# A second form of the products, in four 32-column tiles, where TensorE already stands in column tiles

## The chip, the cores and the metric

The kernel runs on one core of a Trainium2 chip, in one launch. The metric is the device time in microseconds (us). Nine runs of the kernel before gave a median of 564.4 us (563.79 to 564.86).

## The reference, cut to what matters

Two blocks, A (attention with a memory) and B (a dense pair with ReLU), are applied twice to x of 2048 tokens by 640 features, each behind a layer norm and with a residual: `x = x + A(ln(x))`, `x = x + B(ln(x))`, and the same once more.

```
# A: 32 heads of 20, four segments of 512 tokens
q, k, v = x @ wq, x @ wk, x @ wv
for s in range(4):
    p = softmax(q_s @ k_s.T * scale + mask);  a_dot = p @ v_s
    a_mem = (phi(q_s) @ M) / (phi(q_s) @ z + 1e-6)
    o_s = g * a_mem + (1 - g) * a_dot
    M = M + phi(k_s).T @ v_s;  z = z + sum(phi(k_s))
out = concat(o_s) @ wo
# B
out = relu(x @ w1) @ w2          # 640 -> 1728 -> 640
```

`phi(t)` is t + 1 above zero and exp(t) else; the mask keeps a query from later keys.

## The kernel before, in words

All work is cut by the four segments of 512 tokens and the two layers. Every kind of work is a generator of its own (a stream), which yields operations: the scores (`scores`, L1071), their exponentials (`exps`, on ScalarE), the causal cut (`causal`, on GpSimd), the product of the probabilities with the values (`apply`, L1175), the projections (`proj_part`, L783, and `proj_v`, L836), the reading and writing of the memory M (`mem_read`, L971, and `mem_write`, L1022), the output projection (`out_proj`, L1327), and block B (`ffn`, L1381, and `ffn_rest`, L1357). Transposes between them go by DMA (`turn`, L643).

The order on each engine is fixed before the launch by a planner, `Sched` (L169). It holds a modelled clock for each engine. In each step it takes the head of every stream, works out when it could start (`_alts`, L228) and picks the one that can start first, then the one of the better priority (`run`, L267). A TensorE operation carries a modelled duration (`mm_ns`, L346: columns / 2.4 + 2.6 ns) and a form: `full`, `rows` or `cols`. The planner keeps the form in which TensorE stands in `self.mode` and adds `SWITCH_NS` (96 ns, L158) to an operation of another form. An operation with a `lag` (`COLS_LAG`, 1500 ns, L159) is put off in `_late` (L247) as long as the form is `full` and it has not been ready for that long.

The three forms:

- `rows`: the scores (L1093). A head has 20 features, so four heads lie at partitions 0, 32, 64 and 96, and their matmuls use four row groups of the array. 160 such operations, two for each pair of PSUM slots, until all 64 groups of heads are through.
- `cols`: the product with the values (L1187) of four heads and the last 64 columns of w1 (L1367). Each matmul has at most 32 weight columns and writes PSUM partitions 0, 32, 64 or 96 and up; four of them lie side by side in the array. A round is four matmuls, one in each column tile.
- `full`: all the rest, with 128 weight columns. The products go through the helper `group` (L606): k = 0 is L613, the other k are L616, and one operation of the planner is one matmul, so that scores can come between two k. `mem_read` (L984) and `mem_write` (L1036) issue two or three matmuls as one operation. `apply_by_token` (L1226) is the product with the values in the first eight groups, with 21 moving columns.

A matmul in the source is two instructions on TensorE, a weight load (the profile's engine PEld) and the matmul (PE). Only the last matmul of an operation tells a semaphore.

Of the kernel before, what the change touches and what calls it, by code (L numbers as in the profile page):

```python
# [109 lines left out]
class Op:  # L110
# [4 lines left out]
    def __init__(self, alts, waits, dma=None, acq=None, urgent=False, take=(), mode="full", lag=0.0, port=False):  # L115
        self.lag = lag
        self.port = port
        self.alts = alts
        self.mode = mode
        self.acq = acq  # L120
        self.waits = [t for t in waits if t is not None]
        self.dma = dma
        self.urgent = urgent
        self.take = take
# [44 lines left out]
class Sched:  # L169
# [54 lines left out]
    def _pick(self, slots):  # L224
        return min((s for s in slots if s.free), default=None,
                   key=lambda s: max([self.at(t) for t in s.tks], default=0.0))

    def _alts(self, op):  # L228
        res = []
        waits = op.waits  # L230
        if op.acq is not None:
            s = self._pick(op.acq)
            if s is None:
                return res
            waits = waits + s.tks
        for k, (e, hold, fns, tail) in enumerate(op.alts):
            m = PE_MARGIN if e == "pe" else 0.0
            if e == "pe" and op.mode != self.mode:
                hold = hold + SWITCH_NS
            start = max([self.at(t) + SEM_NS + m for t in waits], default=0.0)  # L240
            start = max(self.free[e], start)
            if e == "dve" and op.port and self.free["pool"] > start:
                hold = max(hold, self.free["pool"] - start + PORT_NS)
            res.append((start + hold, start, k, e))
        return res
# [21 lines left out]
    def run(self):  # L267
        while True:
# [40 lines left out]
            _, st, end, start, k, op = best  # L309
            e, hold, fns, tail = op.alts[k]  # L310
            if e == "pe":
                self.mode = op.mode
            waits, slot = op.waits, None
            for s in op.take:
                s.free = False
# [25 lines left out]

def pe(ns, fns, waits=(), acq=None, take=(), mode="full", lag=0.0):
    return Op([("pe", ns, fns, 190.0)], waits, acq=acq, take=take, mode=mode, lag=lag)


def mm_ns(n):  # L346
    return max(26.0, n / 2.4 + 2.6)
# [29 lines left out]
def bass_interleave_layers__memory_aug_infini_attn__dense_activation_relu__prompt_kernel(  # L377
    nc, A_x, A_wq, A_wk, A_wv, A_wo, A_beta, B_x, B_w1, B_w2, out,
):
    with contextlib.ExitStack() as es:  # L380
# [225 lines left out]
        def group(slots, n, mms, waits):  # L606

            bk = tk = None
            last = len(mms) - 1
            for k, (a, b, *w) in enumerate(mms):  # L610
                w = list(w[0]) if w else []
                if k == 0:
                    bk, tk = yield pe(mm_ns(n), [(lambda e, bk, a=a, b=b: e.matmul(  # L613
                        bk.ap[:, 0:n] if len(b.shape) == 2 else bk.ap[:, 0:n].rearrange("p (i n) -> p i n", n=128), a, b, start=True, stop=(last == 0)), last == 0)], list(waits) + w, acq=slots)
                else:
                    tk = yield pe(mm_ns(n), [(lambda e, k=k, a=a, b=b, bk=bk: e.matmul(  # L616
                        bk.ap[:, 0:n] if len(b.shape) == 2 else bk.ap[:, 0:n].rearrange("p (i n) -> p i n", n=128), a, b, start=False, stop=(k == last)), k == last)], w)
            return bk, tk


# [208 lines left out]
        def vx(a, s):  # L829

            return 2 if (a, s) == (0, 0) else s % 2
# [139 lines left out]
        def mem_read(hb):  # L971
            def f(a, s):
# [6 lines left out]
                lst = [(c, max(CH_H0[c], 16 * hb), min(CH_H1[c], 16 * hb + 16)) for c in range(FC)]  # L979
                lst = [x for x in lst if x[1] < x[2]]  # L980
                for i in range(NJ):
                    fns = []
                    for z, (c, h0, h1) in enumerate(lst):
                        fns.append((lambda e, bk, c=c, h0=h0, h1=h1, z=z, i=i: e.matmul(  # L984
                            bk.ap[:, (h0 - 16 * hb) * 21:(h1 - 16 * hb) * 21],
                            phs[:, c * L + i * 128:c * L + (i + 1) * 128],
                            BD[:, CH_OFF[c] + (h0 - CH_H0[c]) * 21:CH_OFF[c] + (h1 - CH_H0[c]) * 21],
                            start=(z == 0), stop=True, skip_group_check=True), z == len(lst) - 1))
                    bk, tk = yield pe(60.0 * len(lst), fns, phi + bdt, acq=MISC if (a, s) == (0, 1) else MISC[:1])
                    rm = yield Acq(RMEM[hb])  # L990
                    om = bk.ap[:, 0:336].rearrange("p (h e) -> p h e", e=21)
                    ta = yield dve(16, 1, lambda e, rm=rm, om=om: e.tensor_scalar(
# [29 lines left out]
        def mem_write(a, s):  # L1022
            mg = yield Need("maskg")
            if s < NSEG - 1:
# [3 lines left out]
                for p, cs in enumerate(PARTS):  # L1028
# [2 lines left out]
                    w = CH_OFF[cs[-1] + 1] - o0  # L1031
                    bk = None
                    for i in range(NJ):
                        fns = []
                        for c in cs:
                            fns.append((lambda e, b=None, c=c, i=i, o0=o0, st=(i == 0 and c == cs[0]), bk=bk: e.matmul(  # L1036
                                (b or bk).ap[:, CH_OFF[c] - o0:CH_OFF[c + 1] - o0], phk[:, c, i, :],
                                VAUG[vx(a, s)][:, i, CH_H0[c]:CH_H1[c], :].rearrange("p h e -> p (h e)"),
                                start=st, stop=True, skip_group_check=True), i == NJ - 1 and c == cs[-1]))
                        if i == 0:  # L1040
                            bk, lastd = yield pe(66.0 * len(cs), fns, pht + vt, acq=MISC)
                        else:
                            lastd = yield pe(66.0 * len(cs), fns)
                    if s == 0:
                        tu = yield dve(w, 1, lambda e, bk=bk, o0=o0, w=w: e.tensor_copy(
                            M_sb[:, o0:o0 + w], bk.ap[:, 0:w]), [lastd] + S.events.get(("BD", a - 1, NSEG - 2), []))
# [468 lines left out]
```

## Time and profile before

| | us |
|---|---|
| median of nine runs | 564.4 |
| the profiled execution | 565.46 |
| its span, first to last instruction | 563.7 |
| TensorE matmuls busy, 5212 of them | 554.3 |
| weight loads busy, 5212 | 298.2 |
| VectorE busy | 410.1 |
| ScalarE busy | 410.9 |
| GpSimd busy | 193.2 |
| products of `group` with w2, 320 columns (L616, x768), busy | 124.3 |
| products of `group` with w1, 512 columns (L616, x416), busy | 113.6 |

Times in the profile are those of one execution. PE is TensorE's matmuls, PEld its weight loads, DVE is VectorE, ACT is ScalarE, POOL is GpSimd, SP issues most DMAs. A row of a group names line, engine, operation, what is written and read, and the shape of one; 128\*32 means 128 rows and 32 weight columns, 128x512 means 128 partitions by 512 columns that stream through. Matmuls are pipelined: a duration holds the way through the array and several matmuls are under way at once. How dense they lie is read from the starts of one and the next in the timeline. In the section on DMA queues a row has packets, MB and share. The chain that ended last is followed back from the last instruction, at each step to what released it.

### The profile page before, as it was taken

Reading aid. Unit: us, or ns where it says so; the run is one execution under the profiler, and the core shown is the slowest. Engines: PE = TensorE matmul, PEld = TensorE weight load, DVE = VectorE, ACT = ScalarE, POOL = GpSimd, SP = SyncE. Lnnn points to the kernel's source line nnn. Section 1 sums busy time; section 2 is a strip of 40 time slices with the busy share of each in tenths; the row PEclk is TensorE's granted clock in tenths of the full one; section 3 lists DMA queues with packets and bytes.
Section 4 is the critical chain, followed back from the end, with each engine's and each line's share of the span. In section 5 each row is a group of like instructions: output and inputs, shape, how many; then the busy total and the mean of one; then the engine's idle time right before and its main releaser. Section 6 shows DMA issues by size and latency. Waiting matters only on the chain.

```text
span 563.7 us, 12825 instructions
## 1 busy us (share of the span) xinstructions
PE 554.3 (98%) x5212; PEld 298.2 (53%) x5212; DVE 410.1 (73%) x1054; ACT 410.9 (73%) x522; POOL 193.2 (34%) x302
## 2 busy tenths in 40 slices
PE   8998999999999999999999999999999999999998
PEld 7554554455554445645445544465445654655655
DVE  4967988998998788899588985588867876452202
ACT  5699889889779878797799787678877678323140
POOL 5345334333444344344333442044421433101000
PEclk9999999999999999999999999999999999999999
DMA  8596998845374417363277141871329311532101
GB/s 267 129 229 162 220 192 190 227 87 89 74 173 90 85 51 162 60 127 53 75 171 139 20 68 37 200 131 28 56 67 215 80 44 20 93 67 59 37 0 48
DMA packets 129980, 60.92 MB, mean 108 GB/s; under 512 B 108802, under 2 KB 119810, under 8 KB 129922
## 3 DMA queue, kind: packets, MB, share of 16 engines
q1 hardware_dynamic: 129504, 59.62, 47.3%
q8 instruction: 41, 0.67, 0.5%
q10 hardware_dynamic: 418, 0.49, 0.3%
q14 instruction: 17, 0.14, 0.1%
HBM read 20.57 MB, written 12.85 MB: 59 GB/s over the span
## 4 chain that ended last, share of the span: by engine, by line
PE 84%; DVE 6%; DMA 5%; ACT 2%; SPq 1%; issue 1%; POOL 0%
PE ps L616 55%; PE ps L613 11%; PE ps L1093 8%; PE ps L1187 6%; DMA otk<-otu 2%; PE ps L984 1%; PE ps L1036 1%; DMA pad<-scr 1%; PE ps L1226 1%; ACT PT L1155 1%; DVE o_sb L1281 1%; PE ps L1367 1%; DMA x_sb<-in_A_x_dram 1%; DVE stats L624 1%; DMA beta_bc<-in_A_beta_dram 1%
## 5 line engine op out<-in xcount | busy, mean ns | idle before, releaser
L1155 ACT ACTIVATE PT<-ps 128x1024 bf16<-128x1024 f32 x320 | 309.0, 1026 | 59.7 <-PE ps L1093 53.7
L1167 POOL TENSOR_SCALAR_AFFINE_SELECT PT<-PT 128x512 bf16<-128x512 bf16 x256 | 167.7, 673 | 265.5 <-ACT PT L1155 265.5
L616 PE MATMUL ps<-w_r,hT 128*128 128x320 bf16 x768 | 124.3, 299 | 0.0
L616 PE MATMUL ps<-xnT,w_r 128*128 128x512 bf16 x416 | 113.6, 379 | 0.0
L1309 DVE TENSOR_TENSOR x_sb<-x_sb,ps 128x320 bf16<-128x320 bf16 x128 | 60.7, 480 | 71.2 <-PE ps L616 70.1
L616 PEld LDWEIGHTS ps<-w_r,hT 128*128 128x128 bf16 x768 | 72.5, 98 | 33.1 <-issue 5.8
L1093 PE MATMUL ps<-pad 20*128 20x512 bf16 (+3 forms) x1024 | 63.4, 301 | 1.9 <-DMA pad<-scr 0.9
L616 PEld LDWEIGHTS ps<-xnT,w_r 128*128 128x128 bf16 x416 | 39.3, 98 | 43.0 <-issue 3.9
L624 DVE BATCH_NORM_STATS2 stats<-x_sb 128x6 f32<-128x320 bf16 x124 | 55.5, 473 | 3.5 <-DMA x_sb<-in_A_x_dram 3.0
L1396 ACT ACTIVATE hT<-ps 128x512 bf16<-128x512 f32 x56 | 33.5, 599 | 22.7 <-PE ps L616 22.1
L616 PE MATMUL ps<-wo_r,oT 128*128 128x320 bf16 x256 | 46.2, 300 | 0.0
L1093 PEld LDWEIGHTS ps<-pad 20*128 20x128 bf16 x1024 | 17.9, 92 | 52.5 <-ACT PT L1155 26.2
L1394 DVE TENSOR_SCALAR hT<-ps 128x512 bf16<-128x512 f32 x48 | 32.7, 683 | 11.7 <-PE ps L616 11.5
L1187 PE MATMUL ps<-PT,v_aug 128*21 128x128 bf16 (+3 forms) x896 | 40.5, 301 | 0.0
L613 PE MATMUL ps<-xnT,w_r 128*128 128x512 bf16 x104 | 39.6, 381 | 0.3 <-DVE om_sb L995 0.3
L1197 DVE CAST otu<-ps 128x512 bf16<-128x512 f32 x46 | 31.4, 682 | 9.0 <-PE ps L1187 8.7
L640 POOL TENSOR_TENSOR rstd<-lnU,mhalf 128x2 f32<-128x2 f32 (+2 forms) x26 | 20.6, 791 | 46.1 <-DVE lnU L636 35.9
L616 PE MATMUL ps<-wv_r,xnT 128*128 128x320 bf16 x192 | 36.2, 300 | 0.0
L616 PE MATMUL ps<-xnT,wk_r 128*128 128x512 bf16 (+1 forms) x128 | 34.9, 366 | 0.0
L616 PE MATMUL ps<-xnT,wq_r 128*128 128x512 bf16 (+1 forms) x128 | 34.0, 366 | 0.0
L950 ACT ACTIVATE stg<-stg 128x512 bf16<-128x512 bf16 x50 | 31.4, 634 | 3.4 <-DVE rtmp L948 3.4
L951 DVE TENSOR_TENSOR phs<-stg,rtmp 128x512 bf16<-128x512 bf16 x50 | 23.7, 474 | 10.3 <-ACT stg L950 9.6
(108 smaller groups left out, 683.1 us busy)
## 6 DMA issues: line engine op xcount, KB each, us to landing
pad<-scr SPq DMA_DIRECT2D x124, 80.0 KB
scr<-stg SPq DMA_DIRECT2D x34, 256.0 KB, 3.0
out_dram<-x_sb SPq DMA_DIRECT2D x16, 160.0 KB, 1.8
w_r<-in_B_w_dram SPq DMA_DIRECT2D x10, 216.0 KB, 2.7
w_r<-in_B_w_dram SPq DMA_DIRECT2D x13, 160.0 KB, 3.0
x_sb<-in_A_x_dram SPq DMA_DIRECT2D x10, 160.0 KB, 3.6
scr<-w_r SPq DMA_DIRECT2D x5, 256.0 KB, 3.0
wv_r<-in_A_wv_dram SPq DMA_DIRECT2D x1, 800.0 KB, 8.4
```

Of the source, the lines that this page charges most:

```text
L613: bk, tk = yield pe(mm_ns(n), [(lambda e, bk, a=a, b=b: e.matmul(bk.ap[:, 0:n] if len(b.shape) == 2 else bk.ap[:, 0:n].rearrange("p (i n) ...
L616: tk = yield pe(mm_ns(n), [(lambda e, k=k, a=a, b=b, bk=bk: e.matmul(bk.ap[:, 0:n] if len(b.shape) == 2 else bk.ap[:, 0:n].rearrange("p (i ...
L624: tk = yield dve(320, 1, lambda e, c2=c2: e.bn_stats(stats6[:, t % 12, c2, :], x_sb[:, t, c2 * 320:(c2 + 1) * 320]), xt)
L950: te = yield act(512, lambda e, q=q: e.activation(q, q, ACT.Exp), [tr] + p, psum=False)
L1093: fns.append([(lambda e, z=z, j=j, hh=hh, N=N, o=o, sl=sl, q=hh % 2: e.matmul(slot.ap[:, q, o:o + N], sl.ap[32 * hh:32 * hh + DH, z, 0, 12 ...
L1155: tx = yield act(1024, lambda e, dst=dst, src=src: e.activation(dst, src, ACT.Exp, scale=SCALE), sc + pw)
L1167: tm = yield pool(600.0, lambda e, reg=reg: e.affine_select(out=reg, in_=reg, pattern=[[0, 4], [1, 128]], compare_op=ALU.is_ge, fill=0.0, ...
L1187: fns.append((lambda e, OD, j=j, hh=hh: e.matmul(OD.ap[32 * hh:32 * hh + DH + 1, 128 * j:L], VAUG[vx(a, s)][:, j, 4 * g + hh, :], pt.ap[:, ...
L1197: te = yield evac(L, 1, lambda e: e.tensor_copy(dst, OD.ap), lambda e: e.activation(dst, OD.ap, ACT.Copy), [tk] + OTU[0].tks)
L1309: ta = yield dve(320, 1, lambda e: e.tensor_tensor(x_sb[:, t, 320 * hf:320 * hf + 320], x_sb[:, t, 320 * hf:320 * hf + 320], bk.ap[:, 0:32 ...
L1394: th = yield evac(512, 1, lambda e, dc=dc, bk=bk: e.tensor_scalar(hT[:, dc, :], bk.ap[:, :], 0.0, None, ALU.max), lambda e, dc=dc, bk=bk: ...
L1396: lambda e, dc=dc, bk=bk: e.activation(hT[:, dc, :], bk.ap[:, :], ACT.Relu), [tk] + HT.tks)
```

## The change

The planner's operation gets a second list of instructions, `cols`. An operation that has one has no form of its own: `_mode` gives it the form in which TensorE stands, unless that is `rows`, where it is `full`. So it never counts as a change of form behind a full or a column operation. When the planner takes it while TensorE stands in columns, `op.cols` is issued instead of the full list. `quarters` cuts the 128 weight columns into four of 32 with their 32 PSUM partitions; each quarter is a matmul with all 128 rows and the same moving columns. The products of `group`, `mem_read` and `mem_write` get this second form. `apply_by_token`, the transposes and the scores keep theirs. The planner's duration is the same for both forms, and the semaphore is told by the last quarter.

```diff
--- before.py
+++ after.py
@@ -117,6 +117,7 @@
         self.port = port
         self.alts = alts
         self.mode = mode
+        self.cols = None
         self.acq = acq
         self.waits = [t for t in waits if t is not None]
         self.dma = dma
@@ -225,6 +226,11 @@
         return min((s for s in slots if s.free), default=None,
                    key=lambda s: max([self.at(t) for t in s.tks], default=0.0))
 
+    def _mode(self, op):
+        if op.cols is None:
+            return op.mode
+        return self.mode if self.mode != "rows" else "full"
+
     def _alts(self, op):
         res = []
         waits = op.waits
@@ -235,7 +241,7 @@
             waits = waits + s.tks
         for k, (e, hold, fns, tail) in enumerate(op.alts):
             m = PE_MARGIN if e == "pe" else 0.0
-            if e == "pe" and op.mode != self.mode:
+            if e == "pe" and self._mode(op) != self.mode:
                 hold = hold + SWITCH_NS
             start = max([self.at(t) + SEM_NS + m for t in waits], default=0.0)
             start = max(self.free[e], start)
@@ -309,7 +315,10 @@
             _, st, end, start, k, op = best
             e, hold, fns, tail = op.alts[k]
             if e == "pe":
+                op.mode = self._mode(op)
                 self.mode = op.mode
+                if op.mode == "cols" and op.cols is not None:
+                    fns = op.cols
             waits, slot = op.waits, None
             for s in op.take:
                 s.free = False
@@ -341,6 +350,15 @@
 
 def pe(ns, fns, waits=(), acq=None, take=(), mode="full", lag=0.0):
     return Op([("pe", ns, fns, 190.0)], waits, acq=acq, take=take, mode=mode, lag=lag)
+
+
+def either(op, cols):
+    op.cols = cols
+    return op
+
+
+def quarters(a):
+    return [(slice(32 * c, 32 * c + 32), a[:, 32 * c:32 * c + 32]) for c in range(4)]
 
 
 def mm_ns(n):
@@ -607,14 +625,29 @@
 
             bk = tk = None
             last = len(mms) - 1
+
+            def view(ap, b):
+                return ap[:, 0:n] if len(b.shape) == 2 else ap[:, 0:n].rearrange("p (i n) -> p i n", n=128)
+
             for k, (a, b, *w) in enumerate(mms):
                 w = list(w[0]) if w else []
+
+                def mm(e, dst, k=k, a=a, b=b):
+                    return e.matmul(view(dst.ap, b), a, b, start=(k == 0), stop=(k == last))
+
+                def quarter(e, dst, rows, part, k=k, b=b):
+                    return e.matmul(view(dst.ap[rows], b), part, b, start=(k == 0), stop=(k == last))
+
                 if k == 0:
-                    bk, tk = yield pe(mm_ns(n), [(lambda e, bk, a=a, b=b: e.matmul(
-                        bk.ap[:, 0:n] if len(b.shape) == 2 else bk.ap[:, 0:n].rearrange("p (i n) -> p i n", n=128), a, b, start=True, stop=(last == 0)), last == 0)], list(waits) + w, acq=slots)
+                    fns = [(mm, last == 0)]
+                    cols = [(lambda e, dst, rows=rows, part=part, q=quarter: q(e, dst, rows, part), last == 0 and c == 3)
+                            for c, (rows, part) in enumerate(quarters(a))]
+                    bk, tk = yield either(pe(mm_ns(n), fns, list(waits) + w, acq=slots), cols)
                 else:
-                    tk = yield pe(mm_ns(n), [(lambda e, k=k, a=a, b=b, bk=bk: e.matmul(
-                        bk.ap[:, 0:n] if len(b.shape) == 2 else bk.ap[:, 0:n].rearrange("p (i n) -> p i n", n=128), a, b, start=False, stop=(k == last)), k == last)], w)
+                    fns = [(lambda e, bk=bk, mm=mm: mm(e, bk), k == last)]
+                    cols = [(lambda e, bk=bk, rows=rows, part=part, q=quarter: q(e, bk, rows, part), k == last and c == 3)
+                            for c, (rows, part) in enumerate(quarters(a))]
+                    tk = yield either(pe(mm_ns(n), fns, w), cols)
             return bk, tk
 
 
@@ -979,14 +1012,19 @@
                 lst = [(c, max(CH_H0[c], 16 * hb), min(CH_H1[c], 16 * hb + 16)) for c in range(FC)]
                 lst = [x for x in lst if x[1] < x[2]]
                 for i in range(NJ):
-                    fns = []
+                    fns, cols = [], []
                     for z, (c, h0, h1) in enumerate(lst):
-                        fns.append((lambda e, bk, c=c, h0=h0, h1=h1, z=z, i=i: e.matmul(
-                            bk.ap[:, (h0 - 16 * hb) * 21:(h1 - 16 * hb) * 21],
-                            phs[:, c * L + i * 128:c * L + (i + 1) * 128],
-                            BD[:, CH_OFF[c] + (h0 - CH_H0[c]) * 21:CH_OFF[c] + (h1 - CH_H0[c]) * 21],
-                            start=(z == 0), stop=True, skip_group_check=True), z == len(lst) - 1))
-                    bk, tk = yield pe(60.0 * len(lst), fns, phi + bdt, acq=MISC if (a, s) == (0, 1) else MISC[:1])
+                        def mm(e, bk, rows, part, c=c, h0=h0, h1=h1, z=z):
+                            return e.matmul(
+                                bk.ap[rows, (h0 - 16 * hb) * 21:(h1 - 16 * hb) * 21], part,
+                                BD[:, CH_OFF[c] + (h0 - CH_H0[c]) * 21:CH_OFF[c] + (h1 - CH_H0[c]) * 21],
+                                start=(z == 0), stop=True, skip_group_check=True)
+                        qt = phs[:, c * L + i * 128:c * L + (i + 1) * 128]
+                        fns.append((lambda e, bk, mm=mm, qt=qt: mm(e, bk, slice(0, 128), qt), z == len(lst) - 1))
+                        for y, (rows, part) in enumerate(quarters(qt)):
+                            cols.append((lambda e, bk, mm=mm, rows=rows, part=part: mm(e, bk, rows, part),
+                                         z == len(lst) - 1 and y == 3))
+                    bk, tk = yield either(pe(60.0 * len(lst), fns, phi + bdt, acq=MISC if (a, s) == (0, 1) else MISC[:1]), cols)
                     rm = yield Acq(RMEM[hb])
                     om = bk.ap[:, 0:336].rearrange("p (h e) -> p h e", e=21)
                     ta = yield dve(16, 1, lambda e, rm=rm, om=om: e.tensor_scalar(
@@ -1031,16 +1069,22 @@
                     w = CH_OFF[cs[-1] + 1] - o0
                     bk = None
                     for i in range(NJ):
-                        fns = []
+                        fns, cols = [], []
                         for c in cs:
-                            fns.append((lambda e, b=None, c=c, i=i, o0=o0, st=(i == 0 and c == cs[0]), bk=bk: e.matmul(
-                                (b or bk).ap[:, CH_OFF[c] - o0:CH_OFF[c + 1] - o0], phk[:, c, i, :],
-                                VAUG[vx(a, s)][:, i, CH_H0[c]:CH_H1[c], :].rearrange("p h e -> p (h e)"),
-                                start=st, stop=True, skip_group_check=True), i == NJ - 1 and c == cs[-1]))
+                            def mm(e, b, rows, part, c=c, i=i, o0=o0, st=(i == 0 and c == cs[0])):
+                                return e.matmul(
+                                    b.ap[rows, CH_OFF[c] - o0:CH_OFF[c + 1] - o0], part,
+                                    VAUG[vx(a, s)][:, i, CH_H0[c]:CH_H1[c], :].rearrange("p h e -> p (h e)"),
+                                    start=st, stop=True, skip_group_check=True)
+                            end = i == NJ - 1 and c == cs[-1]
+                            fns.append((lambda e, b=None, bk=bk, mm=mm, kt=phk[:, c, i, :]: mm(e, b or bk, slice(0, 128), kt), end))
+                            for y, (rows, part) in enumerate(quarters(phk[:, c, i, :])):
+                                cols.append((lambda e, b=None, bk=bk, mm=mm, rows=rows, part=part: mm(e, b or bk, rows, part),
+                                             end and y == 3))
                         if i == 0:
-                            bk, lastd = yield pe(66.0 * len(cs), fns, pht + vt, acq=MISC)
+                            bk, lastd = yield either(pe(66.0 * len(cs), fns, pht + vt, acq=MISC), cols)
                         else:
-                            lastd = yield pe(66.0 * len(cs), fns)
+                            lastd = yield either(pe(66.0 * len(cs), fns), cols)
                     if s == 0:
                         tu = yield dve(w, 1, lambda e, bk=bk, o0=o0, w=w: e.tensor_copy(
                             M_sb[:, o0:o0 + w], bk.ap[:, 0:w]), [lastd] + S.events.get(("BD", a - 1, NSEG - 2), []))
```

## The prediction

> **What bounds the kernel now.** I read the page first: the shares of the engines, then the chain that ended last.
>
> ```profile
> PE 554.3 (98%) x5212; PEld 298.2 (53%) x5212; DVE 410.1 (73%) x1054; ACT 410.9 (73%) x522; POOL 193.2 (34%) x302
> PE 84%; DVE 6%; DMA 5%; ACT 2%; SPq 1%; issue 1%; POOL 0%
> q8 instruction: 41, 0.67, 0.5%
> ```
>
> TensorE is busy 98% of the span, and 84% of the chain runs through it. Its idle time is 563.7 - 554.3 = 9.4 us, and the waits of TensorE (another view) show no place over 1.6 us. The granted clock is 9 or more in every slice. So what counts is how tightly matmuls follow each other, and that is in the starts, since matmuls overlap and their durations say little. The timeline of TensorE (start us, us, line, what) has all three forms side by side:
>
> ```profile
> 371.77 0.40 PE L1093 MATMUL ps<-pad 20*128 20x384 bf16 x8
> 372.10 0.72 PE L1187 MATMUL ps<-PT,v_aug 128*21 128x512 bf16 x16
> 372.75 0.31 PE L613 MATMUL ps<-wo_r,oT 128*128 128x320 bf16 x1
> 372.90 0.71 PE L616 MATMUL ps<-wo_r,oT 128*128 128x320 bf16 x4
> 373.44 0.30 PE L613 MATMUL ps<-wo_r,oT 128*128 128x320 bf16 x1
> 373.58 0.71 PE L616 MATMUL ps<-wo_r,oT 128*128 128x320 bf16 x4
> 374.12 0.30 PE L616 MATMUL ps<-w_r,hT 128*128 128x320 bf16 x1
> 374.26 0.30 PE L613 MATMUL ps<-wo_r,oT 128*128 128x320 bf16 x1
> 374.49 0.40 PE L1093 MATMUL ps<-pad 20*128 20x512 bf16 x4
> 374.82 0.72 PE L616 MATMUL ps<-wo_r,oT 128*128 128x320 bf16 x4
> ```
>
> Full products of 320 columns follow at 0.54 us for four, 136 ns each (single starts: 135 to 136; of 512 columns 215 to 216, of 147 columns 63 to 69). Where the form changes, time is lost: from the last product at 374.26 to the scores at 374.49 are 0.23 us, 96 ns more than the 136. The trace has 394 changes of form: 152 full to rows, 118 rows to full, 54 columns to full, 42 rows to columns, 20 full to columns, 8 columns to rows. Wherever no semaphore is in between, the start comes 95 to 96 ns later than the last matmul's own width would give (231 against 136, 311 against 216; 151 against 56 after the 128-column matmul that ends L1187). That is a tenth of a microsecond each, some 38 us in all.
>
> The column form stands in the trace too:
>
> ```profile
> 457.54 0.30 PE L616 MATMUL ps<-w_r,hR 128*128 128x320 bf16 x1
> 457.77 0.73 PE L1367 MATMUL ps<-xnT,w_r 128*32 128x256 bf16 x20
> 458.32 0.72 PE L1187 MATMUL ps<-PT,v_aug 128*21 128x512 bf16 x16
> 458.97 0.40 PE L1093 MATMUL ps<-pad 20*128 20x384 bf16 x8
> ```
>
> L1367 is just what the change makes of a product: 128 rows, 32 weight columns, four tiles, new weights for each. Its 20 matmuls are five rounds of four and take 0.55 us to the next column operation. The single starts say how: four within 10 ns, the next four 108 to 109 ns after the first four. The full form at 256 columns has 109 (L616, 23 times). In L1187 a round of 384 columns takes 162 to 163 ns, which is 384 / 2.4 + 2.5. Between L1367 and L1187 nothing is lost, since the form stays.
>
> **The change part by part.**
>
> *Changes of form removed.* After a column operation the products now stay in columns until the next scores. Each of the 54 changes columns to full goes: "columns, full, rows" becomes "columns, rows", one stall of 96 ns instead of two. In the tail (the last scores are at 481.4, the last L1187 at 486.8) no scores come any more, so TensorE stays in columns to the end, and the two L1367 there (495.5, 530.9) lose their change into columns as well. 56 x 96 ns = 5.4 us. The skew of 10 ns at the end of a column run is paid once, as before.
>
> *The products' own pace.* From column operations to the next scores the trace has 597 matmuls of the kinds touched (265 of 512, 252 of 320, 80 of the memory, L984 and L1036), in runs of mostly 8 to 15, and 452 in the tail (322 of 320, 130 of 512): 1049 of 2740 take the new form if the order stays. By the rows of L1367 and L1187 a round costs what the full matmul costs, so I take nothing for them. What the trace doesn't show is this form kept up for long. A 320 product becomes 4 weight loads and 4 matmuls in 136 ns, 34 ns a pair. The nearest row is L1226: 40 pairs at 25 ns each (53.48 to 54.50 in the timeline) right behind a wait that had ended 0.2 us before. From below: nothing is gained, since width / 2.4 is the same. From above: the densest stretch of 100 pairs is 41.04 to 45.27, 4.23 us, 42 ns a pair. Were that the limit, a 320 product would take 169 ns, 33 more: 322 x 33 = 10.6 us in the tail, 252 x 33 = 8.3 us before it; 512 products (216) would not feel it. I take 0, by L1226, and keep the upper end as a rival.
>
> [...]
>
> *Memory products.* 58 of 147 columns, 10 of 168 and 12 of 84 follow a column operation. Their full pace is 64, 72 and 37 ns, so 8 instructions would have to pass in that time. Below: 0, as the last round of L1187 (four of 128 columns) is followed 151 ns later, no more than width and switch. Above: four times L1226's 25 ns, 100 ns a round: 58 x 36 + 10 x 28 + 12 x 63 = 3.1 us. I take 0, the row nearest in shape, and keep 3.1 us in the range.
>
> [...]
>
> *Instruction fetch.* 1049 x 6 = 6300 more instructions for TensorE. 41 fetches of 16 KB carry the 10424 weight loads and matmuls and their waits now, some 256 each; each took 0.9 to 1.5 us. At 17 ns an instruction 256 last 4.4 us, so a fetch still fits. Cover gone, each would cost up to 1 us, 14 of them in the tail. At 374.83 a fetch starts and the matmuls after it keep their 136 ns: it is ahead of need. I take 0.
>
> *The order.* The planner sees no switch cost in columns, and its lag of 1500 ns for column operations holds only in full form; a second column operation in a run may come earlier. A few changes of form more or less: 5 x 96 = 0.5 us either way. ScalarE (104 of 137 us busy in 350 to 487) and VectorE (232 of 270 us in 80 to 350) have room for 1% more pace.
>
> *What comes back as waits.* Between the layers (336 to 361) TensorE waits 1.25 us in four places for DVE and a DMA (0.20, 0.17, 0.33, 0.55). Those chains don't get shorter, and some of what was saved before ends in them. I take 0.5 us.
>
> Sum: -5.4 + 0.5 = **-4.9 us**. The profiled execution took 565.46 us around its span of 563.7; it would be 560.6, span 558.8. The median of the nine runs is 564.4, so the forecast is **559.5**.
>
> **Rivals.**
>
> *A. The gain is swallowed.* Some 40 of the 58 column runs lie before 348, 3.8 us. If the latency between the layers takes all of it, 1.6 us are left: 562.8. For it: the chain runs through DMA otk<-otu at 336.9 (4.8 us) and o_sb after it. Against: TensorE is fed with other work there and shows 1.25 us of idle. With the memory rounds at 100 ns (+3.1) it would be no change, 564 to 565.
>
> *B. Issue becomes the bound, slower.* In columns four times the instructions pass per product; place: the 72 us tail without a break, then each run. It decides from 34 ns a pair on. If 42 ns a pair is all that lasts, the tail alone costs 10.6 us: 564.4 + 10.6 - 4.9 = 570; with the runs before (8.3) and the memory rounds at 169 ns (80 x 104 = 8.3) 587. For it: no stretch of the trace beyond 40 pairs is as dense. Against: L1226, and the four starts within 10 ns.
>
> *C. It does not happen.* If the planner puts a product first after scores, TensorE is in full form and nothing changes: 564.4. Against: 42 of 62 entries into columns come straight from scores.
>
> **How the numbers follow.** Forecast 0.64, its own range 557.5 to 562.6 (a few switches more saved; the memory rounds at 3.1). A 0.13, C 0.03, B 0.20. About 0.2% (1.1 us) is what a measurement can tell from no change: faster, below 563.3, is the forecast and a third of A, 0.68; same 0.12; slower 0.20. The range 557.3 to 566.5 holds the forecast, A, C and the mildest of B, and leaves out most of B: some 8 in 10.
>
> **What would show it.** Right: changes columns to full near 0, columns to rows near 60; in the tail products of 320 columns at 136 ns a round, in fours within 10 ns; TensorE's pairs at about 8400; changes of form some 56 fewer. Wrong: rounds of 320 over 140 ns in the tail (B), gaps of about 1 us every 256 instructions (fetch), memory rounds at 100 ns, or the same starts before 336 to 361 and longer waits in it (A).

## The result and the profile after

The changed kernel takes **559.33 us** (median of 10 runs, 558.27 to 560.05), beside 564.50 us for the kernel before (31 runs, 563.72 to 567.04): the ratio is 0.9901, with a 95% interval of 0.9892 to 0.9910. The profiled execution took 559.42 us around a span of 557.7; before it was 565.46 around 563.7. So 5.2 us went by the medians and 6.0 by the spans of the two profiled executions; 4.9 had been forecast. (One execution on record, the profiled one of e1_order_only, stood at a granted clock of 0.64 and took 803.86 us; without it that kernel's median would be 564.2 instead of 564.35.)

The same three lines of the page as before: TensorE's busy time and instructions, the chain of waits by engine, the queue of the instruction fetches (packets of 16 KB, MB, share).

```profile
PE 547.5 (98%) x8257; PEld 308.4 (55%) x8257; DVE 422.5 (76%) x1077; ACT 400.0 (72%) x499; POOL 194.1 (35%) x302
...
q8 instruction: 65, 1.06, 0.8%
...
PE 90%; DVE 4%; DMA 3%; ACT 1%; SPq 1%; POOL 1%; issue 0%; ACTq 0%
```

TensorE passes 8257 pairs of weight load and matmul instead of 5212, its instructions come in 65 fetches instead of 41, and its share of the chain grew. Busy 98% hides the gain: idle was 9.4 us and is 10.2. What went is time *between* the starts, which the busy time counts as busy. It shows in the timeline of TensorE (start us, us, line, what), behind column operations:

```profile
453.03 0.40 PE L1137 MATMUL ps<-pad 20*128 20x384 bf16 x8
453.36 0.72 PE L1231 MATMUL ps<-PT,v_aug 128*21 128x512 bf16 x16
453.91 1.03 PE L639 MATMUL ps<-xnT,w_r 128*32 128x512 bf16 x16
454.77 0.34 PE L1018 MATMUL ps<-BD,phs 128*32 128x84 bf16 x12
454.95 0.39 PE L639 MATMUL ps<-xnT,w_r 128*32 128x512 bf16 x4
```

L1231 is the apply, L1187 of the kernel before. There the product began 0.65 us after it (372.10 to 372.75); here it begins 0.55 us after it (453.36 to 453.91). It is now L639, four matmuls of 32 columns for one of 128. Sixteen of them, four rounds of 512, take 0.86 us to the next operation, 215 to 216 ns each as in the full form. L1018, a memory read of three chunks, issues 12 matmuls in the 0.18 us that its chunks need anyway.

In the tail no scores come any more, and the columns stay to the end:

```profile
482.00 1.94 PE L639 MATMUL ps<-w_r,hT 128*32 128x320 bf16 x52
483.76 0.31 PE L639 MATMUL ps<-w_r,hR 128*32 128x320 bf16 x4
483.90 1.94 PE L639 MATMUL ps<-w_r,hT 128*32 128x320 bf16 x52
...
489.47 0.31 PE L639 MATMUL ps<-w_r,hR 128*32 128x320 bf16 x4
489.60 0.72 PE L1411 MATMUL ps<-xnT,w_r 128*32 128x256 bf16 x20
...
552.85 1.94 PE L639 MATMUL ps<-w_r,hT 128*32 128x320 bf16 x52
554.62 0.31 PE L639 MATMUL ps<-w_r,hR 128*32 128x320 bf16 x4
```

From 482.00 to 483.90 are 14 rounds of 320 columns (52 + 4 matmuls): 1.90 us, 136 ns a round, the full form's pace. It is the same 70 us later, and L1411 starts without a change of form.

Counted in the trace, the changes of form are 339 instead of 394: none from columns to full (54 before), 55 from columns to rows (8), 105 from full to rows (152), 123 from rows to full (118), 37 from rows to columns (42), 19 from full to columns (20). Where a full or a column run ends, the start still comes 93 to 96 ns later than the last matmul's own width would give; behind scores it is 88 to 101 ns. 55 x 96 ns = 5.3 us. (What a change costs in all is more, 111 ns; see e5_alternate.) The waits of TensorE (what waited for what: us in all, times, longest) moved, and did not grow in sum. Two rows of the kernel before, then five of the changed one, the last from its timeline:

```profile
PE ps L1093 <- DMA pad<-scr: 0.9, 2, 0.5
PE ps L1093 <- ACT PT L1155: 0.8, 2, 0.6
...
PE ps L616 <- POOL mhalf L566: 1.6, 1, 1.6
PE ps L1137 <- DMA pad<-scr: 1.1, 1, 1.1
PE ps L1137 <- ACT PT L1199: 0.9, 2, 0.6
PE ps L636 <- DVE w_r L834: 0.9, 1, 0.9
...
365.93 0.39 PE L1137 MATMUL ps<-pad 20*128 20x512 bf16 x4 [1.13 <-DMA pad<-scr]
```

Added up over the trace (whatever a start is late beyond the width of the matmul before it and the 96 ns of a change), the waits are 10.9 us, against 11.1 before. Of the four waits between the layers (336 to 361) three are gone. The fourth, scores behind pad's DMA, has moved and grown: the same scores waited 0.55 us at 360.80 before and wait 1.20 us at 365.93 now, counted alike (the row shows 1.13, without the part under the matmul before). In sum that is 1.25 us before and 1.20 now.

### The profile page after: what moved, and what is told of

Read it like the earlier page. It is cut to its first block, busy times and chain, and to the rows that moved or that the text cites. A ratio compares the mean times of both kernels' runs of the same rounds, so it can differ in the third digit from the quotient of the medians.

```text
span 557.7 us, 18924 instructions
## 1 busy us (share of the span) xinstructions
PE 547.5 (98%) x8257; PEld 308.4 (55%) x8257; DVE 422.5 (76%) x1077; ACT 400.0 (72%) x499; POOL 194.1 (35%) x302
## 3 DMA queue, kind: packets, MB, share of 16 engines
q8 instruction: 65, 1.06, 0.8%
## 4 chain that ended last, share of the span: by engine, by line
PE 90%; DVE 4%; DMA 3%; ACT 1%; SPq 1%; POOL 1%; issue 0%; ACTq 0%
PE ps L636 44%; PE ps L639 26%; PE ps L1137 9%; PE ps L1231 6%; PE ps L1075 1%; PE ps L1270 1%; PE ps L1018 1%; ACT PT L1199 1%; DMA otk<-otu 1%; DMA pad<-scr 1%; PE ps L1411 1%; DVE stats L657 1%; DVE hT L1438 1%; DVE xn_tok L703 1%; DMA beta_bc<-in_A_beta_dram 1%; POOL rstd L673 0%
## 5 line engine op out<-in xcount | busy, mean ns | idle before, releaser
L636 PE MATMUL ps<-w_r,hT 128*128 128x320 bf16 x470 | 75.1, 300 | 0.0
L636 PE MATMUL ps<-xnT,w_r 128*128 128x512 bf16 x276 | 68.6, 380 | 0.0
L639 PE MATMUL ps<-xnT,w_r 128*32 128x512 bf16 x976 | 59.4, 379 | 0.3 <-DVE hT L1438 0.3
L636 PEld LDWEIGHTS ps<-w_r,hT 128*128 128x128 bf16 x470 | 43.6, 98 | 22.4 <-issue 5.7
L639 PE MATMUL ps<-w_r,hT 128*32 128x320 bf16 x1448 | 55.3, 299 | 0.0
L639 PEld LDWEIGHTS ps<-w_r,hT 128*32 128x32 bf16 x1448 | 38.1, 97 | 10.8 <-DVE x_sb L1353 0.3
L1438 DVE TENSOR_SCALAR hT<-ps 128x512 bf16<-128x512 f32 x57 | 38.9, 684 | 6.3 <-PE ps L636 5.7
L1231 PE MATMUL ps<-PT,v_aug 128*21 128x128 bf16 (+3 forms) x896 | 40.4, 301 | 0.4 <-DVE hT L1438 0.4
L636 PEld LDWEIGHTS ps<-xnT,w_r 128*128 128x128 bf16 x276 | 24.6, 97 | 28.2 <-issue 4.8
L639 PEld LDWEIGHTS ps<-xnT,w_r 128*32 128x32 bf16 x976 | 25.3, 97 | 21.3 <-DVE hT L1438 0.5
L636 PE MATMUL ps<-wv_r,xnT 128*128 128x320 bf16 x180 | 33.9, 300 | 0.0
L834 DVE CAST stg<-ps 128x512 bf16<-128x512 f32 x42 | 28.5, 683 | 6.2 <-PE ps L636 5.6
```

Of the source, the lines that this page charges most:

```text
L636: return e.matmul(view(dst.ap, b), a, b, start=(k == 0), stop=(k == last))
L639: return e.matmul(view(dst.ap[rows], b), part, b, start=(k == 0), stop=(k == last))
L834: te = yield evac(N, 1, lambda e, sg=sg, bk=bk: e.tensor_copy(sg.ap[:, t0:t0 + N], bk.ap[:, 0:N]), lambda e, sg=sg, bk=bk: e.activation(sg ...
L1231: fns.append((lambda e, OD, j=j, hh=hh: e.matmul(OD.ap[32 * hh:32 * hh + DH + 1, 128 * j:L], VAUG[vx(a, s)][:, j, 4 * g + hh, :], pt.ap[:, ...
L1438: th = yield evac(512, 1, lambda e, dc=dc, bk=bk: e.tensor_scalar(hT[:, dc, :], bk.ap[:, :], 0.0, None, ALU.max), lambda e, dc=dc, bk=bk: ...
```

## The experiments

Theory S: what pays is the 55 stalls; the column form itself runs at the full form's pace. Rival O: the planner now believes that TensorE stands in columns, so it puts operations in another order, and the order brings the gain. L636 is the full form of a product, L639 the column form; both plan and form are set at one place in the planner's commit (the two lines at "fns = op.cols").

**The new order alone (e1_order_only).** The plan of the changed kernel, the full form always. By the order of the changed kernel that makes 398 changes of form.

```diff
-                if op.mode == "cols" and op.cols is not None:
-                    fns = op.cols
```

> The changed kernel's plan and order on every engine, but every product is issued in full form, so TensorE changes form 398 times instead of 339. Theory (the gain is the stalls of 96 ns at changes of form): 559.3 + 59 x 0.096 = 565.0 us, within 0.5. Rival (the gain comes from the new order, the planner seeing fewer switches): 559.3, as the changed kernel. Rival (the column form itself is quicker per product): between the two, by less than 96 ns a change.

Measured: 564.35 us, ratio 0.9998 (0.9986 to 1.0009), 0.65 below S's number and just outside its 0.5. The order alone gives nothing: O falls.

**The forms alone (e2_forms_only).** The plan of the kernel before; a product is issued in columns where the engine, as tracked beside the plan, stands in columns. 336 changes.

```diff
-        return self.mode if self.mode != "rows" else "full"
+        return op.mode
...
-                op.mode = self._mode(op)
                 self.mode = op.mode
-                if op.mode == "cols" and op.cols is not None:
+                stands = getattr(self, "stands", "full")
+                if op.cols is None:
+                    self.stands = op.mode
+                elif stands == "cols":
                     fns = op.cols
+                else:
+                    self.stands = "full"
```

> The plan and the order of the kernel before on every engine, but a product is issued in columns when TensorE already stands in columns: 336 changes of form instead of 394. Theory (stalls): 564.5 - 58 x 0.096 = 558.9 us, within 0.7. Rival (order): 564.5, no change from before.

Measured: 561.63 us, ratio 0.9953 (0.9936 to 0.9970): 2.8 us gained where 5.6 were expected. Both were too simple. The 58 stalls went, but half of what they were worth came back. Two places in its profile say where: counted as the 10.9 and 11.1 us above, TensorE waits 7.6 us for VectorE, against 5.4 in the kernel before and 5.6 in the changed one, and the clock falls once. The windows view (window, its length, busy us and instructions of PE, PEld, DVE, ACT, POOL, then granted clock, DMA share, GB/s):

```profile
52.40:56.00 3.60, 3.02 (x61) 1.57 (x61) 2.44 (x8) 3.60 (x5) 2.66 (x5) 1.00 0.62 183
56.00:59.50 3.50, 3.10 (x10) 0.81 (x11) 2.65 (x7) 2.82 (x4) 2.57 (x4) 0.57 0.93 230
59.50:63.00 3.50, 3.50 (x60) 2.14 (x59) 3.15 (x11) 2.70 (x4) 0.64 (x1) 0.94 1.05 275
```

0.57 in the window after a wait of 0.88 us for VectorE: half speed for 3.4 us, some 1.7 us lost. Two of its six runs show this; without them the median is 561.3. So of the 5.2 us some 2 come only with the forms *and* the plan made for them together.

**Another tile shape (e4_two_64_tiles).** Two tiles of 64 columns in place of four of 32. Entered from four tiles of 32, that is a change of shape, though both are column tiles. (In three more places, not shown, the last tile that tells the semaphore is c == 1 instead of c == 3.)

```diff
-    return [(slice(32 * c, 32 * c + 32), a[:, 32 * c:32 * c + 32]) for c in range(4)]
+    return [(slice(64 * c, 64 * c + 64), a[:, 64 * c:64 * c + 64]) for c in range(2)]
```

> The changed kernel's plan and order, but the second form has two tiles of 64 weight columns instead of four of 32. Where the stall belongs to a change of the tile's shape, 32 to 64 columns is a change too, 398 in all: 559.3 + 59 x 0.096 = 565.0. Where it belongs only to going between full and column tiles, 559.3.

Measured: 565.0 us, ratio 1.0011 (1.0002 to 1.0021), S's number: all of the gain is gone. Its timeline:

```profile
455.75 0.73 PE L1411 MATMUL ps<-xnT,w_r 128*32 128x256 bf16 x20
456.41 0.41 PE L639 MATMUL ps<-xnT,w_r 128*64 128x512 bf16 x2
...
457.25 0.72 PE L1231 MATMUL ps<-PT,v_aug 128*21 128x512 bf16 x16
457.90 1.05 PE L639 MATMUL ps<-xnT,w_r 128*64 128x512 bf16 x8
```

0.65 us from the apply to the product (457.25 to 457.90), as in the kernel before, not the 0.55 of the changed kernel. What costs the stall is a change of the tiles' shape; every pair of shapes that follow each other in these kernels shows it (93 to 96 ns, behind scores 88 to 101). This is the sharpest test of S: plan, order and columns are those of the changed kernel, and only the shape differs.

**More changes (e5_alternate).** Every second product that would be in columns is issued full: 1288 changes, 949 more than in the changed kernel.

```diff
                 if op.mode == "cols" and op.cols is not None:
-                    fns = op.cols
+                    self.turn = not getattr(self, "turn", False)
+                    if self.turn:
+                        fns = op.cols
```

> The changed kernel's plan and order, but of the product operations that it issues in columns every second one is issued in full form: 1288 changes of form instead of 339, with the same work. Theory (each change costs a stall of 96 ns on the path): 559.3 + 949 x 0.096 = 650.4 us, within 5. Rival (a change costs only where it meets the scores, the rest is hidden by weight loads): under 600.

Measured: 661.29 us, ratio 1.1718 (1.1703 to 1.1733): 10.9 above S's 650.4 and outside its 5, far from the rival's 600. (661.3 - 559.3) / 949 = 107 ns a change, 11 more than S's 96. The timeline has them singly:

```profile
600.15 0.31 PE L638 MATMUL ps<-w_r,hT 128*128 128x320 bf16 x1
600.39 0.32 PE L641 MATMUL ps<-w_r,hT 128*32 128x320 bf16 x4
600.64 0.31 PE L638 MATMUL ps<-w_r,hT 128*128 128x320 bf16 x1
600.88 0.32 PE L641 MATMUL ps<-w_r,hT 128*32 128x320 bf16 x4
```

0.49 us for a pair of products that take 0.27 in one form: 0.22 for two changes, 110 ns each. The 11 ns are no cost of lone rounds, they stand at every change of the kernel before too, outside the 96. There the first full product behind a change is followed after 146 ns (372.75 to 372.90) and the later ones after 136; in the median of 170 such runs it is 10 ns more. And the four matmuls of a round start over 9 to 10 ns: in a run of rounds the next four start 125 to 126 ns after the last of the four before, so this skew is paid once, at the run's end. Counted from the first start of a run to the first start of the next, less what its matmuls need (columns / 2.4 + 2.5 ns, four side by side counted once), a change takes 111 ns in the median, in the kernel before, in the changed kernel and here. By that 949 changes are 105 us; the waits are 2.9 us shorter (8.0 against 10.9).

**Products only (e7_helper_only).** The memory operations keep the full form only; 350 changes.

```diff
-                    bk, tk = yield either(pe(60.0 * len(lst), fns, phi + bdt, acq=MISC if (a, s) == (0, 1) else MISC[:1]), cols)
+                    bk, tk = yield pe(60.0 * len(lst), fns, phi + bdt, acq=MISC if (a, s) == (0, 1) else MISC[:1])
...
-                            bk, lastd = yield either(pe(66.0 * len(cs), fns, pht + vt, acq=MISC), cols)
+                            bk, lastd = yield pe(66.0 * len(cs), fns, pht + vt, acq=MISC)
...
-                            lastd = yield either(pe(66.0 * len(cs), fns), cols)
+                            lastd = yield pe(66.0 * len(cs), fns)
```

> Only the products of the helper have the second form; the memory products (reading and writing) stay full. 350 changes of form instead of 339. Theory (stalls): 559.3 + 11 x 0.096 = 560.4. Rival (memory rounds in columns are slower than full ones, up to 36 ns each at about 80 rounds): 557 to 559, quicker than the changed kernel.

Measured: 563.42 us, ratio 0.9978 (0.9964 to 0.9992), 4.1 us above the changed kernel; neither number. 11 more changes are 1.06 us, and the waits in its profiled execution (562.09 us) are 1.1 us longer (12.0 against 10.9): together 2.2 of the 2.3 us by which its span is longer. Its median is another 1.3 above that execution, which is not settled. Without memory rounds in columns the kernel is slower, not faster; as the plan differs as well, that alone would not exclude a small cost of them. Their starts in the changed kernel do: 63 to 69 ns apart for 147 columns, as in the full form.

**Columns always (e3_all_columns).** The planner and the issue both take columns for every product, so that full form is left only to what has no other: 12016 column matmuls, 335 changes.

```diff
-        return self.mode if self.mode != "rows" else "full"
+        return "cols"
```

> Every product of the helper and of the memory in columns, behind scores too: 12016 column matmuls instead of 5116, 335 changes of form against 339. Theory (stalls, the form itself is free however long it lasts): 559.3 - 4 x 0.096 = 558.9, and up to 1 us either way for the other order. Rival (issue or instruction fetch becomes the bound when columns are kept up, above all in the first 80 us, where the DMA queues are 0.8 busy): over 563.

Measured: 573.13 us, ratio 1.0162 (1.0137 to 1.0187): the theory's 558.9 missed by 14 us, on the rival's side of 563, although within a run no round is slower (320 columns: 135 to 136 ns). The waits:

```profile
PE ps L1137 <- ACT PT L1199: 5.7, 8, 1.7
...
PE ps L639 <- issue: 1.4, 2, 0.8
```

Scores wait eight times for ScalarE's exponential (0.9 us in the changed kernel). "Columns" in the plan also switches off the lag of 1500 ns that holds a column operation back while TensorE is in full form. Two changes had been mixed; the next two kernels part them.

**Columns always, on the changed kernel's plan (e8_all_columns_same_order).** 334 changes.

```diff
-                if op.mode == "cols" and op.cols is not None:
+                if op.cols is not None:
                     fns = op.cols
```

> The changed kernel's plan and order on every engine, but every product in columns, behind scores too: 12016 column matmuls, 334 changes of form instead of 339. Theory (the form costs nothing, e3_all_columns lost its time through its other plan): 559.3 - 5 x 0.096 = 558.8, within 1. Rival (columns kept up cost time by issue or fetch): over 565, near the 573.1 of e3_all_columns.

**The plan of "columns always", form by where the engine stands (e9_plan_of_all_columns).** 375 changes, 4624 column matmuls; in effect the edits of e2_forms_only and e3_all_columns together.

> The plan and order of e3_all_columns, in which the lag of the column operations never holds, but products behind scores are issued full: 375 changes of form, 4624 column matmuls. Theory (the plan of e3_all_columns is what cost there): 573.1 + 40 x 0.096 = 577 us, within 2. Rival (the columns kept up were the cost): 559.3 + 36 x 0.096 = 562.8.

Measured: 567.21 us for the first, ratio 1.0047 (1.0032 to 1.0062), 7.9 above the changed kernel; 570.02 for the second, ratio 1.0101 (1.0088 to 1.0114), 10.7 above it, between its theory's 577 and its rival's 562.8. The second's 36 more changes are 3.5 us (4.0 at 111 ns), so its plan costs some 7, with the same waits for ScalarE:

```profile
PE ps L1141 <- ACT PT L1203: 5.5, 8, 1.8
```

Four of these eight waits (3.6 us) lie between 114 and 122, and behind them the clock is halved from 120.4 to 127.3; all four executions show a mean granted clock of 0.993 or 0.994. TensorE works 5.6 us of that time, so some 2.8 of the 7 us are the clock's. 7.9 + 7 above 559.3 is 574, beside 573.1 measured for both at once. So a plan that never holds column operations back costs 7 us here; no run parts the lag from the change of form that this plan no longer counts. The other 7.9 us, with the plan held fixed, are the rival's "columns kept up": waits of TensorE in e8_all_columns_same_order, two places of its timeline, and the last row of its windows:

```profile
PE ps L1137 <- DMA pad<-scr: 3.5, 2, 2.0
PE ps L639 <- issue: 2.9, 4, 1.2
```
```profile
15.25 0.50 PE L639 MATMUL ps<-xnT,wq_r 128*32 128x256 bf16 x10 [1.22 <-issue]
...
382.83 0.72 PE L639 MATMUL ps<-w_r,hT 128*32 128x320 bf16 x13
384.40 0.59 PE L639 MATMUL ps<-w_r,hT 128*32 128x320 bf16 x11 [0.85 <-issue]
...
59.50:63.00 3.50, 3.50 (x40) 1.01 (x32) 2.51 (x6) 2.57 (x3) 1.71 (x4) 0.58 1.09 242
```

"issue" is a stall for which no semaphore accounts. At 384.40 it falls *inside* a round: 13 matmuls, a stall, 11 matmuls. There are five of one kind (15.25, 43.06, 314.11, 379.24, 384.40), 3.7 us in all by the starts, and counted in TensorE's stream of instructions they stand at 449, 1729, 14785, 17858 and 18113: apart by multiples of 256, within one. (The fourth of the row, at 97.21, is not of them: it stands at 4178.) That is what one fetch carries: 27006 instructions come in 105 fetches, 257 each, and in the changed kernel TensorE starts 256 instructions, in the mean, from the start of one fetch to that of the next. Each stall ends 1.2 to 1.5 us after the fetch before it was transferred. So these are late instruction fetches; the changed kernel shows no stall over 15 ns at the same multiples. The waits for pad's DMA add 2.4 us (3.5 against 1.1), and the clock is halved from 59.0 to 62.4, again behind a wait of 0.87 us, in five of its six runs (some 1.7 us). 3.7 + 2.4 + 1.7 = 7.8 of the 8.7 us by which this execution's span is longer (566.4 against 557.7); its median is 7.9 above.

**Where the fetches are late.** Around 314 and 379 transposing DMAs are under way (oT<-o_sb from 310.20 to 314.87, phk<-phs from 373.06 to 379.80); beside the fetch of 384.40 (381.7 to 382.9) only plain copies are. Four more kernels use plain copies in place of all transposing ones, which leaves the transposition out; their times are compared only with each other.

```diff
-            tk = yield dma("sp", slot_sem, 32768 * n, lambda e: e.dma_start_transpose(dst, src), waits,
+            tk = yield dma("sp", slot_sem, 32768 * n, lambda e: e.dma_start(dst, src.rearrange("p (b n) -> p b n", n=128)), waits,
```

p0_changed_plain is the changed kernel with that; p8_all_columns adds the edit of e8_all_columns_same_order. p11_form_by_stretch chooses the form after the plan is made, for each stretch between two scores: all products in columns if the stretch has a column operation of its own, else all full (320 changes, 5968 column matmuls). p13_columns_after_first has every product full until the first column operation at 79 us and in columns from there (320 changes too, 10784 column matmuls). The core of the choice in p11_form_by_stretch:

```diff
+            own = {m for _, _, m, c in stretch if c is None}
+            form = lambda mode: mode == "cols" if "full" in own else "cols" in own
```

> The changed kernel with its transposing DMAs replaced by plain copies of the same size, so the transposition is left out and the numbers it computes are others; plan, order and all of TensorE's instructions are those of the changed kernel (339 changes of form). It is the base for the three others of this kind. Theory and rival alike: TensorE's work is the same, the copies land sooner, so 556 to 559.5 us; call it P.

> As p0_changed_plain (plain copies for the transposing DMAs), the form chosen per stretch between two scores: all products in columns where the stretch has a column operation of its own, all full else; 320 changes of form instead of 339, 5968 column matmuls instead of 5116. Theory (stalls): P - 19 x 0.096 = P - 1.8 us. Rival (what is saved without a new plan comes back as waits, as in e2_forms_only): P - 0.8 to P.

> As p0_changed_plain, full up to the first column operation at 79 us, from there every product in columns: 320 changes of form, 10784 column matmuls. Theory (columns lose only at single late instruction fetches, most of them in the first 80 us): P - 1.8 and up to 2 us of late fetches, P to P + 0.5. Rival (a loss in proportion to the column matmuls issued, from the 8.4 us of e8_all_columns_same_order): P - 1.8 + 0.82 x 8.4 = P + 5.

> As p0_changed_plain, every product in columns from the start: 334 changes of form, 12016 column matmuls. Theory: the stalls of 1.4 and 0.5 us at instruction fetches in the first 50 us come back, with the waits behind them and the halved clock: P + 3 to P + 6. If the late fetches need the transposing DMAs beside them, they are gone here: P - 0.5. Rival (proportion): P + 8.

Measured: 557.71 us for p0_changed_plain (557.21 to 558.17, four runs), which is P; 555.49 for p11_form_by_stretch (555.28 to 556.38), P - 2.2, where 19 fewer changes make 1.8; 556.08 for p13_columns_after_first (556.03 to 556.34), P - 1.6; 558.57 for p8_all_columns (557.48 to 560.64), P + 0.9. The rivals' losses in proportion (P + 5, P + 8) are far off. p13_columns_after_first is below its theory's range too, since the late fetches allowed for did not come, and p8_all_columns lies between its two theories. Waits of p8_all_columns:

```profile
PE ps L639 <- issue: 1.1, 1, 1.1
```

The two at 320 changes differ by 0.6 us, though one issues almost twice the column matmuls; that is no more than the spread of one of them (1.1), so columns kept up cost little here or nothing. p13_columns_after_first has 98 fetches and none is late. In p8_all_columns, stalls remain only at stream positions 449, 1729 and 1986 (1.24, 0.17, 0.24 us), in the first 50 us; those after 300 us, the waits for pad and, but for one of six runs (560.64), the halved clock are gone. So the late fetches after 300 us and, of these kernels, the 4 us of clock and pad come only with columns everywhere *and* the transposing DMAs together. Whether it is the transposition or what the queues then hold and when isn't told apart by this; the one at 384.40, with plain copies beside its fetch, speaks for the second. The choice by stretch points beyond the changed kernel (2.2 us of 557.7). With the transposing DMAs in place no run measures it, nor columns from the first column operation on, nor a tail in full form.

## Why the prediction came true, point by point

- **Changes of form.** The mechanism is the one forecast: 56 changes fewer were foreseen and 55 are counted. e4_two_64_tiles and e5_alternate carry it: put the change of shape back and the gain is gone; add 949 changes and the time grows with them. The price was read too low. "95 to 96 ns" is what lies between a run's last start and the next (88 to 101 behind scores); with the slower first product and the skew a change takes 111 ns. 55 x 111 = 6.1 us, and the spans differ by 6.0.
- **The products' own pace.** Taken as 0, with 42 ns a pair as the upper end. Measured: 34 ns a pair in every run of 320-column rounds of the tail, 44 us of its 73, up to 15 us without a break (509.8 to 524.8).
- **Memory products.** Taken as 0 (upper end 3.1 us). Measured: 63 to 69 ns for 147 columns, 36 to 40 for 84, as in the full form. Four loads and four matmuls do fit into 37 ns.
- **Instruction fetch.** Taken as 0; right for this change, with 65 fetches and no late one. The reason given, "at 17 ns an instruction 256 last 4.4 us, so a fetch still fits", was too wide: e8_all_columns_same_order has the same density for longer and loses 3.7 us to late fetches. The cover is there for runs of some microseconds, in a tail with quiet queues (DMA share 0.24 there), and in p13_columns_after_first with its plain copies, not everywhere.
- **The order.** "A few changes of form more or less: 5 x 96 = 0.5 us either way." The number of changes came out that way (1049 products in columns foreseen, 1015 found), but the plan does more than that: e1_order_only shows it worth nothing by itself, and e2_forms_only that without it some 2 us of the gain are lost again in waits and the clock. That interplay is in no term of the sum.
- **What comes back as waits.** 0.5 us was taken off; between the two profiled executions the waits shrank by 0.2 instead. That and the 0.7 us by which the changes were priced too low (6.1 for 5.4) are the 1.1 us between the span forecast (558.8) and the one measured (557.7), within 0.3. By the medians 5.2 us went, 0.9 less than the changes are worth, and no trace shows where: the profiled execution of the kernel before is 1.0 us above its median. So that 4.9 came so near to 5.2 is in part luck: the price was 0.7 too low, the 0.5 of waits is not seen in the traces, and the 0.9 that the medians lack makes up for most of both.
- **The rivals.** A named 336 to 361 as the place where the gain would end. One of its waits did grow, by 0.65 us, now at 365.93; the other three went, and in sum nothing of the gain ended there. B's place was the tail, at 34 ns a pair: refuted there; stalls at late fetches show only in kernels that issue far more columns. C fell with the first column product behind an apply.

## What to carry to other kernels

On an engine that is busy all the time, read the starts, not the busy time: a change of the tiles' shape costs a fixed stall (111 ns here, 96 of them between the last start and the next), and an operation that can take the shape its neighbour already has removes it at no price in pace (136 ns for a product of 320 columns in both forms). Do not carry the shape further than that: columns everywhere saved hardly any more changes and lost 8 us, beside transposing DMAs, in late instruction fetches, DMA waits and the clock. And let the planner know of the choice, since half the gain of the forms came back in waits and at a halved clock when the order was not made for them.

## What the runs showed of the hardware that was not expected

- From tiles of 32 columns to tiles of 64, and from those to scores, the start comes 93 to 96 ns late (e4_two_64_tiles), as from columns to full.
- TensorE's instructions arrive in blocks of 256 (27006 in 105 fetches in e8_all_columns_same_order, whose five stalls stand apart by multiples of 256, within one). A late block stopped it for 0.2 to 1.4 us, at 384.40 inside a round.
- In e2_forms_only the granted clock was halved for 3.4 us (0.57 in the window from 56.0 to 59.5) behind a wait of only 0.88 us. The same wait, for the write of w_r, stands in the changed kernel (55.71) without that. The traces say what goes with it. In the four profiled executions where it happens, the halving begins a whole number of steps of 3.413 us after the clock's rise at the start: 15 in e2_forms_only (5.31 to 56.51), 16 in e8_all_columns_same_order, 35 in e3_all_columns, 34 in e9_plan_of_all_columns. The step is in the traces without a halving inside as well: from rise to fall the full clock lasts 552.96 us in the changed kernel and 556.37 in the kernel before, 162 and 163 steps. Matmuls streamed (columns / 2.4 ns each, overlaps counted once) for 0.41, 0.42, 0.19 and 0.29 of the step before it. Of the 1801 steps at full clock in eleven traces these four have the lowest shares, a kernel's last step aside (0.00 in the changed kernel, 0.22 in the kernel before; the clock falls behind it too); the next is 0.46. In e2_forms_only the wait fell into one step with 40 narrow matmuls (L1274, 21 columns every 25 ns); in the changed kernel a step's boundary at 53.5 parted such a run of 40, and the step with the wait has 0.53. So whether the same wait halves the clock seems to hang on where the steps fall; no run was made to test this.
